# Half of chunk 1's h by seven half-size products, with weight sums moved to GpSimd

## The chip, the cores and the metric

The kernel runs on one core of one Trainium2 chip. The metric is the device time of that core in microseconds; the kernel before takes 255.4 us, the median of 3 runs that lie between 255.4 and 255.65. A profile is one further execution, recorded by the hardware.

Engine names in the profile: PE is TensorE (PEld its weight loads), DVE is VectorE, ACT is ScalarE, POOL is GpSimd, SP is SyncE, which issues most transfers.

## The reference

Linear attention for 8 batches of 8 heads, 576 rows and 64 columns, and a two-layer network on its result:

```
q_s = softmax(q, axis=-1);  k_s = softmax(k, axis=2)        # q, k, v: (8, 8, 576, 64)
kv  = einsum('bhsd,bhse->bhde', k_s, v)
x   = einsum('bhsd,bhde->bhse', q_s, kv) -> (4608, 512)
h   = x @ w_in                                              # w_in: (512, 2048)
g   = 0.5 * h * (1 + erf(h / sqrt(2)))
out = g @ w_out                                             # w_out: (2048, 512)
```

## The kernel before, in words

**Chunks.** The 576 rows of each batch are cut into 512 and 64. Chunk c (0 to 7) is the 512 rows of batch c; chunk 8 is the 64 rest rows of all batches. A chunk passes through: exponentials of q and k on ScalarE (`exp_q`, `exp_k`), casts of v to bf16 (`cast_v`), 72 small products for kv (`kv_mm`), the scaling of q by its sums (`norm_q`, or `q_sums` and `q_scale` apart), a transposition of q (from batch 2 on by a transposing DMA, `xbar_step`), the product x (`x_mm`, evacuated to `xT`), then h (L393 or L513), gelu, and y (L799).

**h.** xT has 512 contraction rows (4 blocks of 128) and 512 tokens; h has 16 tiles of 128 features, in the program's order t. In a *plain* tile (`h_mm`, `h_gelu`) four products of 512 columns go to one PSUM bank, and one ScalarE gelu moves it to `g`. Tiles t and t + 8 make a pair. Chunks 0 and 1 are all plain. From chunk 2 on, `h_waves` makes h in four groups (q = 0 to 3) of two pairs each by Strassen's scheme in Winograd's form: seven products of half the rows and half the tokens instead of eight. A product is four instructions of 256 columns. It needs sums of blocks of xT (`x_sums`, t1 to t4, on VectorE), sums of blocks of w_in made once (`quad_weights`, s1 to s4 for each half of the groups), and sums of the products:

- mm(1) into bank A, copied on as C (`seed`); mm(5) into bank B, copied to SBUF as r (`p5_copy`)
- mm(6) added to A; `e_sum`: B = A + r on VectorE; mm(2) added to C, whose gelu follows
- mm(7) added to A, after `e_sum` has read A; `r_sum`: r = A + r on VectorE, whose gelu follows
- mm(3) added to B, mm(4) to A after `r_sum` has read A; gelus of A and B

**y.** It uses the same scheme on g and w_out. Sums of blocks of g (`s_parts` and `s_ops`, VectorE) are made as pairs become ready; the mixed blocks of w_out (`mix_wo`, blocks 1, 3, 4, 6 and 7, each in two halves) once. `y_phase` runs seven products of 16 instructions in the order 4, 5, 1, 2, 3, 6, 7 (from chunk 2 on 3 follows 4; from chunk 3 to 7 product 3 is again split, class `Two`, whose weights are made by `weights(0)` and `weights(1)` on GpSimd). Between its products stand the steps of later batches, given as lists by place.

**Order.** Each engine runs its instructions in the order in which the program records them; the order is written out by hand. Semaphores make an instruction wait for what it reads or overwrites, and what is behind it on its engine waits too.

**Around the change.** In chunk 1 (L1150 to L1200) four plain tiles (8, 0, 9, 1) are made by hand, beside chunk 0's last evacuations and x. VectorE then mixes four half blocks of w_out (L1168 to L1171). `h_pairs` makes the other six pairs plain, with `s_ops` for every two pairs, and between them the w_in sums of the second half of the groups (`sums[0]` to `sums[2]`) on VectorE and the casts of batch 2's v on ScalarE. Then follow `exp_q(2)` and `exp_k(2)`, and `y_phase(1)`, in which batch 2's q is scaled and transposed, its kv made, batch 3's exponentials taken, and chunk 2's x made. Chunk 2's `h_waves` has `q_late` in its middle, which scales batch 3's q on GpSimd, issues its transposition and makes `weights(1)`.

Of the kernel before, what the change touches and what calls it, by code (L numbers as in the profile page):

```python
# [16 lines left out]
def kernel(  # L17
# [20 lines left out]
    J = 4  # L38
# [119 lines left out]
                in_=q[b, :, M:S, :].rearrange("h p d -> p h d"),  # L158
            )

    def exp_q(b, parts=1):

        e = attn_sb.tile([128, J, H, D], BF16, tag="eq")
        st[b]["eq"] = e
        dst = e.rearrange("p j h d -> p h j d")
        src = st[b]["qf"]
        if b == B:
            src = src.rearrange("p j h d -> p h j d")
        else:
            src = src.rearrange("p h (j d) -> p h j d", j=J)  # L170
        if parts == 1:
            sets = [(slice(i, None, 4), slice(u, None, 4)) for i, u in ((0, 0), (1, 1), (2, 3), (3, 2))]
        else:
            sets = []
            for h in (0, 4):
                sets += [(slice(h + i, h + i + n), slice(h + u, h + u + n))
                         for i, u, n in ((0, 0, 2), (2, 3, 1), (3, 2, 1))]
        for i, u in sets:
            nc.scalar.activation(out=dst[:, i], in_=src[:, u], func=AF.Exp)  # L179
# [221 lines left out]
    def s_parts(c, p0, n, which):  # L401


        g = st[c]["g"]
        a, b = slice(p0, p0 + n), slice(p0 + HK, p0 + HK + n)
        lo, hi = slice(0, HT), slice(HT, M)
        tt = nc.vector.tensor_tensor
        if 0 in which:
            tt(out=s5[:, a], in0=g[:, a, lo], in1=g[:, b, lo], op=ALU.add)
        if 1 in which:  # L410
            tt(
                out=s12[:, a].rearrange("p k (u m) -> p k u m", u=2),
                in0=g[:, a].rearrange("p k (u m) -> p k u m", u=2),
                in1=g[:, b, hi].unsqueeze(2).to_broadcast([128, n, 2, HT]), op=ALU.add,
            )
# [3 lines left out]
        if 2 in which:  # L419
            tt(out=g[:, a, hi], in0=g[:, a, hi], in1=g[:, a, lo], op=ALU.subtract)  # L420
            tt(out=g[:, b, lo], in0=g[:, b, lo], in1=g[:, b, hi], op=ALU.subtract)  # L421

    def s_ops(c, p0, n):
# [19 lines left out]
    def tt(out, in0, in1, op=ALU.add, eng=nc.vector):  # L443
        eng.tensor_tensor(out=out, in0=in0, in1=in1, op=op)  # L444

    quad = {"s": {}}

    def quad_weights(w):

        q = quad["s"][w] = wst.tile([128, 4, 2, 512], BF16, tag=("w4", "w1")[w], name="quad_s")  # L450
        up, dn = slice(w * 512, w * 512 + 512), slice((w + 2) * 512, (w + 3) * 512)
        a11, a12 = wi_bf[:, 0:2, up], wi_bf[:, 2:4, up]
        a21, a22 = wi_bf[:, 0:2, dn], wi_bf[:, 2:4, dn]
        s1, s2, s3, s4 = (q[:, i] for i in range(4))
        return [
            lambda: tt(s1, a21, a22), lambda: tt(s2, s1, a11, ALU.subtract),
            lambda: tt(s3, a11, a21, ALU.subtract), lambda: tt(s4, a12, s2, ALU.subtract),
        ]
# [19 lines left out]
    def h_waves(c, mid, sums=None):  # L478

        h_begin(c)
# [9 lines left out]
        if mid:  # L492
            bank_of.update(B=("kv0", "kv1") * 2, C=("x1", "x2") * 2)
        held = {}

        def take(kind, q):
            held[kind, q] = bank(roles[bank_of[kind][q]], "q" + kind.lower(), (128, 2, HT))

        def mm(m, *qs):
            for q in qs:  # L500
# [29 lines left out]
        def r_sum(q):  # L530
            tt(held["r", q], held["A", q], held["r", q])
# [5 lines left out]
                nc.scalar.activation(out=g[:, t:t + 2, half], in_=held[kind, q], func=AF.Gelu)  # L537

        vcopy, scopy = nc.vector.tensor_copy, nc.scalar.copy
        mm(1, 0, 1)  # L540
        seed(0)
        if mid:
# [10 lines left out]
            mm(6, 0, 1)  # L553
            e_sum(0)
            e_sum(1)
            mid()
            mm(2, 2, 3)
            gelu("C", 2, 3)
            mm(7, 0, 1)
            r_sum(0)  # L560
            r_sum(1)
            mm(3, 0, 1)
            gelu("B", 0, 1)
            mm(6, 2)
# [129 lines left out]
    class Two:  # L694
# [11 lines left out]
        def weights(self, part):  # L706

            W = wo_bf[:, UP, HN:DM].rearrange("p (a h b) n -> p h a b n", h=2, b=2)
            b11, b12, b21, b22 = (W[:, i, :, :, j:j + 128] for i in range(2) for j in (0, 128))
            o = [self.w[:, i].rearrange("p (a b) n -> p a b n", b=2) for i in range(5)]  # L710
            eng = nc.gpsimd
            if part == 0:
                tt(o[0], b11, b22, eng=eng)
                tt(o[1], b12, b22, ALU.subtract, eng=eng)
                return
            tt(o[2], b21, b11, ALU.subtract, eng=eng)
            tt(o[3], b11, b12, eng=eng)
            tt(o[4], b21, b22, eng=eng)
            w = self.w[:, 4]
            eng.tensor_scalar(out=w, in0=w, scalar1=-1.0, scalar2=None, op0=ALU.mult)  # L720

# [56 lines left out]
    def y_phase(c, ins, p3=None):  # L778
# [30 lines left out]
        if p3:  # L809
            p3.mm(c, bx, (4, 5, 1), True)  # L810
            p3.snap(bx)
        mm(4, bd, True)
        if c > 1:
            nc.scalar.copy(out=f, in_=bd)
            after(8)
            if p3:
                p3.mm(c, bx, (2, 3, 6, 7), False)
            else:
                mm(3, bx, True)
            nc.scalar.copy(out=c12, in_=two(bx))  # L820
            after(9)
        else:
            nc.vector.tensor_copy(out=f, in_=bd)
        after(0)
        if p3:
            p3.corner2(c12)
# [165 lines left out]

    w16 = None

    def mix_wo(m, a):


        lo, hi = slice(0, HN), slice(HN, DM)
# [10 lines left out]
        nc.vector.tensor_tensor(out=o, in0=i0, in1=i1, op=op)  # L1009

    def warm(n, z):
        ps = psum_y.tile([128, DM], FP32, tag="y")
# [269 lines left out]
```

## Time and profile before

| | |
|---|---|
| median of 3 runs | 255.4 us |
| the profiled execution, its time | 255.87 us |
| its span, first to last instruction | 253.9 us |
| TensorE busy | 247.9 us, 98% |
| VectorE busy | 219.1 us, 86% |
| ScalarE busy | 190.4 us, 75% |
| GpSimd busy | 102.8 us, 40% |
| chunk 1's h, by the chain | 44.1 to 58.5 us |
| y of chunk 1, with batch 2's kv | 58.5 to 71.6 us |
| chunk 2's h | about 72.9 to 85.3 us |

How to read it: the busy share of TensorE counts matmuls whose ends are modelled, so the chain of waits, followed back from the last instruction, says better what holds the end. A line of it has the start, the length, the engine, what was written, the line of the kernel, and how many instructions were merged. In the timeline a line has the start, the time from the first start to the last end, the engine, line, operation, what was written from what, sizes and count; in brackets the idle time before it and what ended it. A line of stretches has, for each engine, busy time and count, then the granted TensorE clock, the share of the DMA engines and GB/s.

### The profile page before, as it was taken

How to read it: one execution, taken by the hardware profiler on the slowest of the kernel's cores; microseconds unless marked ns; L12 is line 12 of the kernel's file. 1: busy time of each engine (PE TensorE's matmuls, PEld its weight loads, DVE VectorE, ACT ScalarE, POOL GpSimd, SP SyncE). 2: the span in 40 equal slices, each digit the busy share in tenths (PEclk: the TensorE clock that was granted, in tenths of full speed). 3: DMA queues.
4: the chain of work that ended last, by engine and by line, in shares of the span. 5: the costliest groups of instructions: out<-in, count | busy, mean ns of one | idle time of the engine just before them, and what ended most of it. 6: DMA issues, size and time to landing. Idle time of an engine off the chain costs nothing.

```text
span 253.9 us, 6825 instructions
## 1 busy us (share of the span) xinstructions
PE 247.9 (98%) x2738; PEld 196.1 (77%) x2738; DVE 219.1 (86%) x395; ACT 190.4 (75%) x326; POOL 102.8 (40%) x177
## 2 busy tenths in 40 slices
PE   7999999999999999999999999999999999999994
PEld 3444444448888888898889988998889889988883
DVE  1878898788987997998999899989999999868972
ACT  4785978699977996889688968896887788248711
POOL 1530023000978459106950596059603960560000
PEclk9999999999999999999999999999999999999998
DMA  7999999995329999890569255810520061004033
GB/s 239 397 367 420 405 406 400 401 407 206 61 64 288 375 265 377 246 340 5 188 196 310 98 188 177 204 36 3 165 87 3 1 193 57 3 4 165 0 84 84
DMA packets 43168, 50.24 MB, mean 198 GB/s; under 512 B 20225, under 2 KB 30465, under 8 KB 42881
## 3 DMA queue, kind: packets, MB, share of 16 engines
q1 hardware_dynamic: 42416, 49.13, 57.8%
q10 hardware_dynamic: 720, 0.69, 1.0%
q8 instruction: 21, 0.34, 0.6%
q14 instruction: 11, 0.08, 0.1%
HBM read 36.70 MB, written 9.44 MB: 182 GB/s over the span
## 4 chain that ended last, share of the span: by engine, by line
PE 81%; DMA 16%; DVE 1%; SPq 0%; issue 0%
PE qa L513 19%; PE ya L799 10%; PE qb L513 10%; PE yd L799 10%; DMA f<-in_q_dram 7%; PE ye L799 6%; PE ps L393 6%; PE yb L799 5%; PE qc L513 5%; DMA w<-in_moe_w_out_dram 3%; DMA w<-in_moe_w_in_dram 3%; PE yx L753 3%; DMA f<-in_v_dram 2%; PE kv L231 2%; PE ps L359 1%; PE ya L882 1%
## 5 line engine op out<-in xcount | busy, mean ns | idle before, releaser
L513 PEld LDWEIGHTS <-quad_s 128*128 128x128 bf16 x448 | 43.8, 98 | 5.1
L799 PEld LDWEIGHTS <-g 128*128 128x128 bf16 x368 | 35.2, 98 | 4.8 <-issue 0.4
L513 PEld LDWEIGHTS <-wi_bf 128*128 128x128 bf16 x336 | 32.8, 98 | 3.9
L799 PEld LDWEIGHTS <-s 128*128 128x128 bf16 x336 | 32.7, 98 | 3.7
L513 PE MATMUL qa<-quad_t,quad_s 128*128 128x256 bf16 x224 | 29.2, 273 | 0.0
L275 POOL TENSOR_TENSOR e<-e,recq 128x1024 bf16<-128x1024 bf16 (+1 forms) x4 | 9.3, 2330 | 47.8 <-DVE recq L270 41.0
L393 PE MATMUL ps<-xT,wi_bf 128*128 128x512 bf16 x128 | 28.1, 379 | 0.2 <-DVE kvc L244 0.2
L444 POOL TENSOR_TENSOR y_sb<-y_sb 128x128 f32<-128x128 f32 x56 | 26.0, 498 | 2.8 <-issue 2.8
L269 DVE TENSOR_REDUCE qsum<-e 128x16 f32<-128x1024 bf16 (+1 forms) x12 | 20.9, 1746 | 6.8 <-ACT e L179 6.5
L284 POOL TENSOR_TENSOR e<-e,recq 128x256 bf16<-128x256 bf16 x40 | 24.7, 653 | 1.8 <-DVE recq L270 1.2
L393 PEld LDWEIGHTS <-wi_bf 128*128 128x128 bf16 x128 | 12.4, 98 | 15.3 <-issue 0.7
L521 ACT COPY qc<-qa 128x512 f32<-128x512 f32 x26 | 13.9, 577 | 11.4 <-PE qa L513 5.3
L399 ACT ACTIVATE g<-ps 128x512 bf16<-128x512 f32 x32 | 17.6, 602 | 6.1 <-PE ps L393 5.8
L179 ACT ACTIVATE e<-f 128x512 bf16<-128x512 f32 (+1 forms) x42 | 20.5, 556 | 2.1 <-DMA f<-in_q_dram 1.9
L537 ACT ACTIVATE g<-r 128x512 bf16<-128x512 f32 x28 | 17.3, 631 | 6.3 <-DVE r L444 6.3
L444 DVE TENSOR_TENSOR qb<-qa,r 128x512 f32<-128x512 f32 x28 | 18.1, 691 | 4.1 <-PE qa L513 1.6
L537 ACT ACTIVATE g<-qc 128x512 bf16<-128x512 f32 x28 | 15.2, 594 | 7.4 <-PE qc L513 7.4
L418 DVE TENSOR_TENSOR s<-g 128x1024 bf16<-128x1024 bf16 x28 | 19.8, 726 | 0.0
L196 POOL CAST v_aug<-f 128x576 bf16<-128x576 f32 x25 | 17.0, 711 | 4.4 <-DMA f<-in_v_dram 4.3
L444 DVE TENSOR_TENSOR r<-qa,r 128x512 f32<-128x512 f32 x28 | 17.9, 680 | 0.7 <-PE qa L513 0.7
L184 ACT ACTIVATE ek<-f 128x2304 bf16<-128x2304 f32 (+1 forms) x10 | 17.2, 1734 | 1.2 <-DMA f<-in_k_dram 1.2
L1213 POOL CAST scr<-g 128x1 f32<-128x1 bf16 x4 | 0.7, 187 | 42.3 <-DVE g L421 42.3
(117 smaller groups left out, 550.2 us busy)
## 6 DMA issues: line engine op xcount, KB each, us to landing
out_dram<-y_sb SPq DMA_DIRECT2D x16, 512.0 KB, 3.9
f<-in_k_dram SPq DMA_DIRECT2D x6, 1152.0 KB, 9.5
f<-in_v_dram SPq DMA_DIRECT2D x6, 1152.0 KB, 10.5
f<-in_q_dram SPq DMA_DIRECT2D x6, 1024.0 KB, 7.6
w<-in_moe_w_in_dram SPq DMA_DIRECT2D x6, 512.0 KB, 8.9
f<-in_v_dram SPq DMA_DIRECT2D x8, 288.0 KB, 6.5
f<-in_q_dram SPq DMA_DIRECT2D x4, 512.0 KB, 9.0
w<-in_moe_w_out_dram SPq DMA_DIRECT2D x2, 1024.0 KB, 11.4
```

What stands on the lines that cost most here:

```text
L179: nc.scalar.activation(out=dst[:, i], in_=src[:, u], func=AF.Exp)
L184: nc.scalar.activation(out=ek[b % 2][:, i:i + n], in_=st[b]["kf"][:, i:i + n].rearrange("p x (n d) -> p x n d", n=NS), func=AF.Exp,)
L196: eng.tensor_copy(out=o, in_=i)
L269: nc.vector.reduce_sum(out=qsum, in_=st[b]["eq"][:, :, i * w:(i + 1) * w, :], axis=AX.X)
L284: nc.gpsimd.tensor_tensor(out=e, in0=e, op=ALU.mult, in1=st[b]["recq"][:, j, i:i + 4].unsqueeze(2).to_broadcast([128, 4, D]),)
L393: nc.tensor.matmul(ps, wi_bf[:, dm, t * 128:(t + 1) * 128], st[c]["xT"][:, dm, :], start=(dm == 0), stop=(dm == NDM - 1),)
L399: nc.scalar.activation(out=st[c]["g"][:, t, :], in_=ps, func=AF.Gelu)
L418: tt(out=s12[:, a, half], in0=g[:, a, half], in1=g[:, b, hi], op=ALU.add)
L444: eng.tensor_tensor(out=out, in0=in0, in1=in1, op=op)
L513: nc.tensor.matmul(held[kind, q][:, u], w, mov[m][:, k], start=(m in (1, 5) and u == 0 and k == 0), stop=(k == 1), skip_group_check=True,)
L537: nc.scalar.activation(out=g[:, t:t + 2, half], in_=held[kind, q], func=AF.Gelu)
L799: nc.tensor.matmul(ps[:, j * HN:(j + 1) * HN], act[m][:, k, j * 128:(j + 1) * 128], wgt[m][:, k, :], start=(first and k == 0 and j == 0), ...
```

## The change

- Chunk 1's tiles 2, 3, 10 and 11 (pairs 2 and 3) stay plain, now inside `h_waves`. Pairs 4 to 7 become groups 2 and 3 of `h_waves`, with the products in the order 5, 1, (plain pair 3), 6, 2, 7, 3, 4.
- All four block sums of w_in for these groups go to GpSimd, each in four pieces of 128x256: sums 0 and 2 ahead of the scaling of batch 1's q, sums 1 and 3 after the last plain tiles made by hand. So do the mixed half blocks 7, 4, 1 and 3 of w_out, in four pieces each, and after them the casts of batch 2's v.
- `x_sums(1)` is made on VectorE. `s_ops` of pairs 2 and 3 stands after plain pair 3, ahead of `e_sum`. The sums of pairs 4 to 7 are made together after the last gelus, one of them (part 6) later in `y_phase(1)`.
- `exp_q(2)` is cut in two halves around the copy of the first y product, which goes from VectorE to ScalarE; `exp_k(2)` follows. In the program they stand inside `y_phase(1)`.
- Batch 3's q is summed and scaled in two halves, the second in chunk 2's `h_waves` after `r_sum(1)`, and then transposed. `weights(1)` goes from `q_late` to the beginning of chunk 3, in pieces of half the size.

```diff
@@ quad_weights(w, parts=None)
+        if parts:
+            def tt(out, in0, in1, op=ALU.add):
+                for k in range(2):
+                    for n in (slice(0, 256), slice(256, 512)):
+                        nc.gpsimd.tensor_tensor(out=out[:, k, n], in0=in0[:, k, n], in1=in1[:, k, n], op=op)
+        else:
+            tt = two_block_sum
@@ h_waves
+        first_banks = {"A": (5, 6), "B": (1, 7), "C": (3, 4)}
+
+        def plain(p):
+            for i, t in ((2, p + HK), (0, p)):
+                ps = bank(i)
+                h_mm(c, ps, t, range(NDM))
+                h_gelu(c, ps, t)
...
+        if c == 1:
+            plain(2)
+            for q in (2, 3):
+                mm(5, q)
+                mm(1, q)
+            seed(2)
+            seed(3)
+            p5_copy(2, vcopy)
+            p5_copy(3, vcopy)
+            plain(3)
+            s_ops(c, 2, 2)
+            mm(6, 2, 3)
+            e_sum(2)
+            e_sum(3)
+            mm(2, 2, 3)
+            gelu("C", 2, 3)
+            mm(7, 2, 3)
+            r_sum(2)
+            r_sum(3)
+            gelu("r", 2, 3)
+            mm(3, 2, 3)
+            mm(4, 2, 3)
+            gelu("A", 2, 3)
+            gelu("B", 2, 3)
+            s_parts(c, 4, 4, (0,))
+            s_parts(c, 4, 4, (3,))
+            s_parts(c, 4, 4, (4,))
+            s_parts(c, 4, 4, (5,))
+            return
...
-            mid()
+            mid[0]()
             mm(2, 2, 3)
             gelu("C", 2, 3)
             mm(7, 0, 1)
             r_sum(0)
             r_sum(1)
+            mid[1]()
@@ Two.weights
-            tt(o[2], b21, b11, ALU.subtract, eng=eng)
-            tt(o[3], b11, b12, eng=eng)
-            tt(o[4], b21, b22, eng=eng)
+            for a in range(2):
+                tt(o[2][:, a], b21[:, a], b11[:, a], ALU.subtract, eng=eng)
+                tt(o[3][:, a], b11[:, a], b12[:, a], eng=eng)
+                tt(o[4][:, a], b21[:, a], b22[:, a], eng=eng)
@@ y_phase
+        if c == 1:
+            exp_q(2, parts=2, part=0)
         mm(4, bd, True)
...
-            nc.vector.tensor_copy(out=f, in_=bd)
+            nc.scalar.copy(out=f, in_=bd)
+            exp_q(2, parts=2, part=1)
+            exp_k(2)
@@ mix_wo(m, a, parts=False)
+        if parts:
+            for i in range(4):
+                nc.gpsimd.tensor_tensor(out=o[:, i], in0=i0[:, i], in1=i1[:, i], op=op)
+        else:
+            nc.vector.tensor_tensor(out=o, in0=i0, in1=i1, op=op)
@@ chunk 1
-    sums = quad_weights(1)
+    sums = quad_weights(1, parts=True)
+    sums[0]()
+    sums[2]()
     mix_wo(6, 0)
...
-    mix_wo(7, 1)
-    mix_wo(4, 1)
-    mix_wo(1, 1)
-    mix_wo(3, 1)
+    sums[1]()
+    sums[3]()
+    for m in (7, 4, 1, 3):
+        mix_wo(m, 1, parts=True)
+    cast_v_all(2)
...
-    h1 = {p + 3: [lambda p=p: cast_v(2, p, nc.scalar)] for p in range(HP)}
-    h1[1] = [sums[0]]
-    h1[3] += sums[1:3]
-    h_pairs(1, h1, done=t1s, turn=Banks(2, 0, 5, 6))
-
-
-    exp_q(2, parts=2)
-    exp_k(2)
+    x_sums(1, (1, 2, 3, 4))
+    s_ops(1, 0, 2)
+    h_waves(1, None)
...
     y_phase(1, {
-        0: [sums[3]],
         7: [lambda: norm_q(2, 0, 2)],
-        1: [lambda: norm_q(2, 1, 2, nc.vector)],
+        1: [lambda: norm_q(2, 1, 2, nc.vector), lambda: s_parts(1, 4, 4, (6,))],
         2: [lambda: cast_v_all(3), first_weights, lambda: xbar_step(2), lambda: exp_q(3)],
-        3: [lambda: kv_step(2), lambda: exp_k(3), lambda: q_sums(3)],
+        3: [lambda: kv_step(2), lambda: exp_k(3), lambda: q_sums(3, 0, 2)],
...
-        q_scale(3, nc.gpsimd)
+        q_scale(3, nc.gpsimd, 0, 2)
+
+    def q_later():
+        norm_q(3, 1, 2)
         xbar_step(3)
-        y3.weights(1)
...
-        h_waves(c, q_late if c == 2 else None, p3 and p3.sums)
+        if c == 3:
+            y3.weights(1)
+        h_waves(c, (q_late, q_later) if c == 2 else None, p3 and p3.sums)
```

More of the change, by code (lines that the diff above doesn't have):

```diff
@@ L159, in load_qrest, with exp_q @@
             )
-    def exp_q(b, parts=1):
-        e = attn_sb.tile([128, J, H, D], BF16, tag="eq")
-        st[b]["eq"] = e
+    def exp_q(b, parts=1, part=None):
+        if part != 1:
+            st[b]["eq"] = attn_sb.tile([128, J, H, D], BF16, tag="eq", name="e")
+        e = st[b]["eq"]
         dst = e.rearrange("p j h d -> p h j d")
@@ L174, in exp_q @@
             sets = []
-            for h in (0, 4):
+            for h in (0, 4) if part is None else (4 * part,):
                 sets += [(slice(h + i, h + i + n), slice(h + u, h + u + n))
@@ L418, in s_parts @@
                 tt(out=s12[:, a, half], in0=g[:, a, half], in1=g[:, b, hi], op=ALU.add)
-        if 2 in which:
+        if 2 in which or 5 in which:
             tt(out=g[:, a, hi], in0=g[:, a, hi], in1=g[:, a, lo], op=ALU.subtract)
+        if 2 in which or 6 in which:
             tt(out=g[:, b, lo], in0=g[:, b, lo], in1=g[:, b, hi], op=ALU.subtract)
@@ L444, in tt, with quad_weights @@
         eng.tensor_tensor(out=out, in0=in0, in1=in1, op=op)
+    two_block_sum = tt
     quad = {"s": {}}
-    def quad_weights(w):
+    def quad_weights(w, parts=None):
         q = quad["s"][w] = wst.tile([128, 4, 2, 512], BF16, tag=("w4", "w1")[w], name="quad_s")
@@ L478, in h_waves @@
     def h_waves(c, mid, sums=None):
-        h_begin(c)
+        if c > 1:
+            h_begin(c)
         g, xT = st[c]["g"], st[c]["xT"]
@@ L494, in h_waves @@
         held = {}
+        first_banks = {"A": (5, 6), "B": (1, 7), "C": (3, 4)}
[4 more added lines that the diff above has]
+                h_gelu(c, ps, t)
         def take(kind, q):
-            held[kind, q] = bank(roles[bank_of[kind][q]], "q" + kind.lower(), (128, 2, HT))
+            i = first_banks[kind][q - 2] if c == 1 else roles[bank_of[kind][q]]
+            held[kind, q] = bank(i, "q" + kind.lower(), (128, 2, HT))
         def mm(m, *qs):
@@ L993, with mix_wo @@
     w16 = None
-    def mix_wo(m, a):
+    def mix_wo(m, a, parts=False):
         lo, hi = slice(0, HN), slice(HN, DM)
@@ L1008, in mix_wo @@
         }[m]
-        nc.vector.tensor_tensor(out=o, in0=i0, in1=i1, op=op)
+        if parts:
[3 more added lines that the diff above has]
+            nc.vector.tensor_tensor(out=o, in0=i0, in1=i1, op=op)
     def warm(n, z):
```

## The prediction

> **What bounds the kernel now.** I read the page first, then the chain of waits in order of time, then the timeline of the stage that changes.
>
> ```profile
> PE 247.9 (98%) x2738; PEld 196.1 (77%) x2738; DVE 219.1 (86%) x395; ACT 190.4 (75%) x326; POOL 102.8 (40%) x177
> PE 81%; DMA 16%; DVE 1%; SPq 0%; issue 0%
> ```
>
> The chain that ends last is 81% TensorE. In order of time it leaves DMA and VectorE at 44.12 us and then holds TensorE alone to 250.34:
>
> ```profile
> 45.48 13.06 PE ps L393 x60
> 58.54 1.75 PE yd L799 x16
> ...
> 63.78 1.75 PE yd L799 x16
> 65.52 0.76 PE kv L231 x72
> ...
> 75.67 0.87 PE qb L513 x8
> 76.55 0.87 PE qa L513 x8
> ```
>
> So behind 44 us a product saved is time saved, and every gap that opens on TensorE is time lost: nothing hides it. Eight products of 256 columns take 0.87 us (0.109 each); the 60 of 512 columns are 0.216 apart by their starts.
>
> The stage in question on the other engines (start, duration, then the work):
>
> ```profile
> 51.67 0.60 ACT L399 ACTIVATE g<-ps 128x512 bf16<-128x512 f32 x1 [0.27 <-PE ps L393]
> 52.30 0.43 DVE L409 TENSOR_TENSOR s<-g 128x512 bf16<-128x512 bf16 x1 [0.48 <-ACT g L399]
> 52.64 0.68 DVE L411 TENSOR_TENSOR s<-g 128x1024 bf16<-128x1024 bf16 x1
> 53.36 0.42 DVE L420 TENSOR_TENSOR g<-g 128x512 bf16<-128x512 bf16 x1
> 53.70 0.42 DVE L421 TENSOR_TENSOR g<-g 128x512 bf16<-128x512 bf16 x1
> 54.03 0.68 DVE L444 TENSOR_TENSOR quad_s<-quad_s,wi_bf 128x1024 bf16<-128x1024 bf16 x1
> ```
> ```profile
> 59.19 1.28 ACT L179 ACT_TABLE_LOAD   x1
> 60.48 2.38 ACT L179 ACTIVATE e<-f 128x512 bf16<-128x512 f32 x6
> 62.76 2.11 ACT L184 ACTIVATE ek<-f 128x2304 bf16<-128x2304 f32 x1
> 65.45 0.83 PE L231 MATMUL kv<-v_aug,ek 64*64 64x65 bf16 x72
> 77.17 1.29 DVE L444 TENSOR_TENSOR qb<-qa,r 128x512 f32<-128x512 f32 x2
> ```
>
> To see: the four VectorE sums of one pair of plain tiles start 0.03 us after the tile's gelu and hold VectorE for 1.73 us (52.30 to 54.03); exp_k(2) ends at 64.87, only 0.58 us ahead of the kv products that read it.
>
> **The change part by part.** Terms are in us against the profiled execution (span 253.9, time 255.87, so 1.97 lie around the span); its time is 0.47 over the median 255.4, and I put the sum on the median.
>
> *1. Products.* Tiles of pairs 4 to 7 were 8 x 4 products of 512 columns, 32 x 0.216 = 6.91. They become two groups of seven products in four pieces, 56 x 0.109 = 6.12. **-0.8**.
>
> *2. mm(7) waits for e_sum behind s_ops.* The new VectorE order is s_ops(1,2,2), then e_sum(2), e_sum(3). mm(7) adds into the bank that e_sum reads, so it waits. TensorE before: the first product of the last 60 starts at 45.41. After: 20 products of 512 to 49.74, four groups of four halves (4 x 0.437) to 51.49, plain(3) (8 x 0.216) to 53.21, mm(6) and mm(2) (2 x 0.874) to 54.96, where mm(7) would start. VectorE: plain(3)'s last product starts at 53.00 and runs 0.38, its gelu follows 0.04 later (both as the tile ahead of the gelu at 50.80 shows), 53.41 to 54.01; the four sums run 54.05 to 55.78 (1.73 as above), e_sum(2) 0.69 to 56.47, TensorE 0.07 behind it: 56.54. Lost 1.58, and 0.16 more, as e_sum(3) ends 0.60 later and half of mm(7) takes 0.44. **+1.74**. Queued behind mm(7) on TensorE is everything that follows.
>
> *3. GpSimd beside those sums.* GpSimd gets 8 + 16 more pieces of 128x256 from 42.4 on (its last cast of v_aug now ends at 42.38). The nearest rows are its e pieces of the same shape, 8 in 4.80, 0.6 each, so it works till 56 at least, over both s_ops. What such pieces do to a VectorE sum with both inputs in SBUF:
>
> ```profile
> 94.28 4.80 POOL L284 TENSOR_TENSOR e<-e,recq 128x256 bf16<-128x256 bf16 x8 [0.57 <-ACT ek L184]
> 97.62 0.42 DVE L444 TENSOR_TENSOR quad_t<-xT 128x512 bf16<-128x512 bf16 x1
> 98.77 0.60 DVE L444 TENSOR_TENSOR quad_t<-xT,quad_t 128x512 bf16<-128x512 bf16 x1
> ```
>
> 0.00 and 0.18 over the 0.42 that it takes alone; in later chunks the same sums beside the same pieces take 0.60 to 0.89, +0.47 at most. Four sums stand ahead of e_sum: 0 to 1.9; I take 0.28 each, the middle of what is seen, **+1.1**. The Trainium skill (SBUF — State Buffer, "Who interferes with whom") goes further: a VectorE instruction with two SBUF inputs and a GpSimd one that reads SBUF exclude each other for whole instructions. By that each sum could wait for a whole piece, 4 x 0.6 = 2.4, and the total would be 260.3; the 0.42 row agrees less than the 0.89 ones. x_sums(1) meets the pieces too, but has 47.6 against 49.7 to spare. GpSimd's own results come in time: mixed block 4 ends near 54 (used from 57), block 3 near 59 (used at 67), cast_v(2) near 63 (used at 67).
>
> *4. exp_k(2) comes late.* ACT must first finish gelu A and B of groups 2 and 3, which need mm(4), the last product ahead of the y stage (start T). By the pitch of 0.55 for such gelus the last ends at T+1.9. Then the table (1.28), half of exp_q(2) (1.14), the copy of yd, now ACT's (0.47 until the next starts), the other half (1.14), exp_k (2.11): T+8.1. TensorE reaches kv at T + 64 x 0.109 = T+7.0 (before: 65.45 with T 58.4). **+1.15**, with 1.0 to 1.4 as ends. The copy of yd ends at T+4.9, just ahead of mm(2) at T+5.2, which writes that bank. Behind, ACT needs 6.56 from exp_k's end to the end of the next gelu table (64.87 to 71.43), TensorE 6.1 from kv to the x products and 0.5 to their end: no second gap. norm_q(2) ends near T+9.5 and its transposing DMA (2.27 at 66.64) at T+12, for x products at T+14. Where this stall goes, nothing else is late by these rows.
>
> *5. Sums 0 and 2 of w_in on GpSimd at 30.4 to 36.* GpSimd idled 19.96 there. Beside it VectorE has three sums and a cast, then a q scaling that must wait for GpSimd's own (it took 1.72 beside one, 1.23 alone): about +1.4 at 38.1. VectorE idled 1.04 and 0.19 for DMA at 40.36 and 40.98, and its work from there is on the chain until 44.08. Ends 0 and 0.6; **+0.25**.
>
> *6. VectorE and ACT freed.* Four mixes (0.69 each), four w_in sums, and four v casts on ACT (0.66) go. None was on the chain: nothing, since TensorE covers it.
>
> *7. Batch 3's q.* q_sums(3) in halves: the second (1.22 + 0.25) falls in chunk 2 where VectorE idled 1.46 ahead of e_sum: 0 to 0.1, nothing taken. The scaling on GpSimd (3.62) becomes 2 x 1.90, the second from 81.6, so the transposing DMA is issued about 3 us later than at 80.75; it took 9.24 beside 3 loads, and x needs it 95.7. The loads behind it on SP (90.03) are for the next batch's exp, 20 us later. Nothing; without that cover at most 3.
>
> *8. y3's weights(1) in chunk 3.* Six pieces and 1.49 from 102.8 to about 109, used at 111.1. They lie beside five VectorE sums ahead of e_sum, up to 0.3 each, against slack of 0.36 idle and 0.30 to mm(7): 0 to 0.7, **+0.15**.
>
> Sum: -0.8 + 1.74 + 1.1 + 1.15 + 0.25 + 0.15 = +3.6; 255.4 + 3.6 = **259.0**.
>
> **The rivals.**
>
> *Faster.* If mm(7) found its e_sum done at 54.96 and kv its exp_k at T+7, only term 1 is left: 254.6. That needs e_sum 1.6 us earlier than VectorE's order allows, or ACT 1.1 us shorter. For it: VectorE and ACT lose work in this stage, and both waits are worked out, not seen. Against it: VectorE is in order, and the gelu it waits for is itself behind TensorE, so a late or early stage moves both ends together. 0.05; a mix that ends within 0.5 us of before, 0.03.
>
> *One wait alone.* Terms 2 and 3 without 4 and the small ones: 255.4 - 0.8 + 2.8 = 257.4; bare term 2 alone: 256.3; term 4 alone, 255.8, which is no change. For it: terms 3, 5 and 8 rest on contention that some rows do not show. 0.12.
>
> *Whole pieces.* Each of the four sums waits for one whole GpSimd piece of 0.6: 259.0 - 1.1 + 2.4 = 260.3. For it the rows of 0.89, against it the row of 0.42 beside a piece. 0.12. (It is what the Trainium skill's rule in term 3 gives.)
>
> *The clock.* A gap of 2.8 us on TensorE has no example between 44 and 250 us, but the end has one:
>
> ```profile
> 250.30:252.00 1.70, 0.02 (x1) 0.00 (x0) 0.29 (x1) 0.00 (x0) 0.00 (x0) 1.00 0.66 162
> 252.00:253.90 1.90, 0.00 (x0) 0.00 (x0) 0.00 (x0) 0.00 (x0) 0.00 (x0) 0.63 0.21 50
> ```
>
> The granted clock (third figure from the end) averages 0.63 in the last stretch, so it fell to half some 2.1 us after the last product. If it falls in the gap, and stays for as long as it was low at the start at most (products from 1.44; 5 us), half of that is lost: 259.0 + 2.6 = 261.6. The Trainium skill (TensorE: Matmul & The Clock Gate, Part 1) asks for an idle window of about 3.4 us first, which speaks against it here; the 2.1 us speak for it. 0.10.
>
> **How the numbers follow.** Forecast 0.58; whole pieces 0.12; the clock 0.10; one wait alone 0.12; within 0.2% 0.03; faster 0.05. 0.2% is 0.5 us, about what a measurement of this kernel can tell from no change. Faster 0.05, same 0.03, slower 0.92. The forecast's own ends: low 255.4 - 0.8 + 1.74 + 0 + 1.0 = 257.3, high with 1.9, 1.4, 0.6 and 0.7 260.9. The range reaches to the middle of one wait alone below, 256.9, and to 261.2 above.
>
> **What would show it.** In the changed profile's chain: products of chunk 1 end 0.8 earlier by their sum; TensorE idle of 1.7 to 3.6 ahead of the second qa of groups 2 and 3, released by VectorE qb; idle of about 1.15 ahead of the kv products, released by ACT ek; s_ops rows over 0.42 and 0.68 beside GpSimd; granted clock at 1.00 there. The prediction is wrong if e_sum runs ahead of s_ops(1,2,2), if mm(7) starts within 0.5 us of mm(2)'s end, or if ek ends before TensorE has reached kv.

## The result, and the profile after

The changed kernel takes 263.5 us (median of 4 runs, 261.9 to 263.9) against 255.4 (4 runs, 255.38 to 255.65): a ratio of 1.030, 95% interval 1.026 to 1.035. So it is slower, by 8.1 us where 3.6 were forecast. The profiled execution took 263.85 us, with a span of 262.0. Now and then an execution takes about twice as long, whatever the kernel (519.6 us was seen); such executions are in none of the times here.

The page of the changed kernel, busy times, the granted clock in 40 slices, and the chain by engine:

```profile
PE 249.0 (95%) x2757; PEld 198.7 (76%) x2762; DVE 228.6 (87%) x391; ACT 190.2 (73%) x325; POOL 134.2 (51%) x217
PEclk9999997999999999999999999999999999999999
PE 82%; POOL 5%; ACT 5%; DMA 4%; DVE 2%; issue 1%; SPq 0%; POOLq 0%; ACTq 0%
```

GpSimd and ScalarE were not on the chain before; now they hold 5% each. DMA's 16% on the old chain is 4%: the work ahead of 44 us ends last on another engine. The clock dips in the seventh slice, at 39 to 46 us.

The chain of waits of the changed kernel, in order of time, at the places where it is not TensorE:

```profile
30.56 5.82 POOL quad_s L463 x6
36.66 1.29 POOL quad_s L463 x2
37.95 2.84 POOL e L276
40.79 2.15 POOL v_aug L197 x2
...
61.14 0.62 DVE qb L446
61.81 0.61 PE qa L533 x4
...
70.58 2.02 ACT ek L185
72.64 0.83 PE kv L232 x71
```

Three places: GpSimd's new sums of w_in ahead of chunk 1, e_sum ahead of mm(7), exp_k(2) ahead of kv. A table of TensorE's landmarks, by the starts of its instructions, shows what each is worth:

| us | before | after | lost there |
|---|---|---|---|
| first of the long run of 512-column products in chunk 1's h | 45.41 | 49.01 | 3.60 |
| first product of y | 58.37 | 64.58 | 2.61 |
| batch 2's kv | 65.45 | 72.64 | 0.98 |
| chunk 2's h | 72.81 | 80.00 | 0.00 |
| chunk 3's h | 98.72 | 105.94 | 0.03 |
| x products of chunk 4 | 121.36 | 129.38 | 0.80 |
| span | 253.9 | 262.0 | 0.08 |

The first row is the surprise. The changed kernel's timeline of that stage (start, duration, then the work), VectorE and then GpSimd:

```profile
31.07 1.69 DVE L1044 CAST wo_bf<-w 128x2048 bf16<-128x2048 f32 x1
32.80 2.11 DVE L1068 TENSOR_TENSOR w<-wo_bf 128x1024 bf16<-128x1024 bf16 x2
38.95 3.45 DVE L1068 TENSOR_TENSOR wo_bf<-wo_bf 128x1024 bf16<-128x1024 bf16 x2
42.33 1.69 DVE L1044 CAST wo_bf<-w 128x512 bf16<-128x512 f32 x2
...
30.56 7.39 POOL L463 TENSOR_TENSOR quad_s<-wi_bf 128x256 bf16<-128x256 bf16 x8 [15.31 <-ACT wo_bf L1046]
37.91 2.88 POOL L276 TENSOR_TENSOR e<-e,recq 128x1024 bf16<-128x1024 bf16 x1
40.74 3.00 POOL L197 CAST v_aug<-f 128x576 bf16<-128x576 f32 x3
```

The same instructions in the kernel before:

```profile
30.99 1.22 DVE L989 CAST wo_bf<-w 128x2048 bf16<-128x2048 f32 x1
32.25 1.29 DVE L1009 TENSOR_TENSOR w<-wo_bf 128x1024 bf16<-128x1024 bf16 x2
38.04 1.28 DVE L1009 TENSOR_TENSOR wo_bf<-wo_bf 128x1024 bf16<-128x1024 bf16 x2
35.14 1.90 POOL L275 TENSOR_TENSOR e<-e,recq 128x1024 bf16<-128x1024 bf16 x1 [19.96 <-DVE recq L270]
```

Each is longer beside the other engine, and each makes the next overlap that was not there: the eight pieces take 7.39 us, so GpSimd's scaling of q starts 2.77 us later and takes 2.88 for 1.90; it holds VectorE's mixes (3.45 for 1.28); then the casts of v lie beside the casts of w_out. TensorE, which has only short work here (transpositions, 64-wide kv products), waits three times for GpSimd, 2.0 us in all; its timeline in the changed kernel:

```profile
40.84 0.71 PE L324 MATMUL tp<-identity,e 64*64 64x64 bf16 x64 [0.82 <-POOL e L276]
41.91 0.22 PE L232 MATMUL kv<-v_aug,ek 64*64 64x65 bf16 x2 [0.36 <-POOL v_aug L197]
42.98 0.61 PE L232 MATMUL kv<-v_aug,ek 64*64 64x65 bf16 x34 [0.86 <-POOL v_aug L197]
```

Then its clock falls to half, for 3.4 us. Stretches of the changed kernel (the third figure from the end is the granted clock):

```profile
43.10:44.80 1.70, 1.48 (x37) 0.81 (x34) 1.70 (x6) 0.13 (x1) 1.70 (x3) 0.51 1.05 411
44.80:46.50 1.70, 1.70 (x5) 0.44 (x3) 0.89 (x3) 0.19 (x1) 1.70 (x4) 0.50 1.04 411
```

Three of the kernels below have the same work and much the same waits here, and in their profiles the clock does not fall. One of them, with exp_k(2) moved:

```profile
41.80:43.90 2.10, 0.89 (x58) 0.63 (x46) 2.10 (x3) 1.58 (x2) 2.10 (x3) 1.00 1.09 398
43.90:46.50 2.60, 2.60 (x48) 1.35 (x48) 2.60 (x8) 1.10 (x3) 2.60 (x5) 1.00 1.04 411
```

In these three the long run starts 6.66 us after the first transposition, in the changed kernel 8.17, in the kernel before 5.46. So the fall of the clock is 1.5 of the 3.60 us, and the waits are the other 2.1.

The stage that the prediction was about, again from the timeline of the changed kernel: plain(3)'s gelu, the four sums, e_sum, the pieces on GpSimd beside them, and the product that waits; then exp_k(2) and kv.

```profile
57.01 0.60 ACT L400 ACTIVATE g<-ps 128x512 bf16<-128x512 f32 x1 [0.27 <-PE ps L394]
57.64 0.81 DVE L410 TENSOR_TENSOR s<-g 128x512 bf16<-128x512 bf16 x1
58.38 1.15 DVE L412 TENSOR_TENSOR s<-g 128x1024 bf16<-128x1024 bf16 x1
59.56 0.77 DVE L421 TENSOR_TENSOR g<-g 128x512 bf16<-128x512 bf16 x1
60.26 0.88 DVE L423 TENSOR_TENSOR g<-g 128x512 bf16<-128x512 bf16 x1
58.13 3.54 POOL L1066 TENSOR_TENSOR wo_bf<-wo_bf 128x256 bf16<-128x256 bf16 x4
61.81 1.20 PE L533 MATMUL qa<-quad_t,quad_s 128*128 128x256 bf16 x8 [3.08 <-DVE qb L446]
...
70.48 2.11 ACT L185 ACTIVATE ek<-f 128x2304 bf16<-128x2304 f32 x1
72.64 0.83 PE L232 MATMUL kv<-v_aug,ek 64*64 64x65 bf16 x72 [0.91 <-ACT ek L185]
```

The sums are the forecast ones in the forecast place: 3.43 us from the first to e_sum's start, against 1.73 alone. Each takes 0.35 to 0.47 us more than its 0.42 or 0.68. e_sum, which reads one of its inputs from PSUM, takes its usual 0.69 beside a piece.

### The profile page after: what moved, and what is told of

Same layout as the page of the kernel before. It is cut to its first block, busy times and chain, and to the rows that moved or that the text cites. A ratio compares the mean times of both kernels' runs of the same rounds, so it can differ in the third digit from the quotient of the medians.

```text
span 262.0 us, 6914 instructions
## 1 busy us (share of the span) xinstructions
PE 249.0 (95%) x2757; PEld 198.7 (76%) x2762; DVE 228.6 (87%) x391; ACT 190.2 (73%) x325; POOL 134.2 (51%) x217
## 4 chain that ended last, share of the span: by engine, by line
PE 82%; POOL 5%; ACT 5%; DMA 4%; DVE 2%; issue 1%; SPq 0%; POOLq 0%; ACTq 0%
PE qa L533 19%; PE qb L533 10%; PE ya L850 9%; PE yd L850 8%; PE ps L394 8%; PE ye L850 5%; PE yb L850 5%; PE qc L533 5%; PE yx L804 3%; POOL quad_s L463 3%; PE kv L232 2%; DMA f<-in_v_dram 2%; PE ps L360 2%; DMA f<-in_q_dram 2%; PE ya L937 1%; POOL v_aug L197 1%
## 5 line engine op out<-in xcount | busy, mean ns | idle before, releaser
L533 PEld LDWEIGHTS <-quad_s 128*128 128x128 bf16 x480 | 46.9, 98 | 10.0 <-issue 4.1
L533 PE MATMUL qa<-quad_t,quad_s 128*128 128x256 bf16 x240 | 31.6, 272 | 3.4 <-DVE qb L446 3.4
L557 ACT ACTIVATE g<-r 128x512 bf16<-128x512 f32 x30 | 18.5, 631 | 10.8 <-DVE r L446 10.8
L557 ACT ACTIVATE g<-qc 128x512 bf16<-128x512 f32 x30 | 16.3, 594 | 8.2 <-PE qc L533 8.2
L197 POOL CAST v_aug<-f 128x576 bf16<-128x576 f32 x29 | 21.0, 758 | 1.1 <-DMA f<-in_v_dram 1.1
L446 DVE TENSOR_TENSOR qb<-qa,r 128x512 f32<-128x512 f32 x30 | 19.4, 690 | 2.1 <-PE qa L533 1.4
L394 PE MATMUL ps<-xT,wi_bf 128*128 128x512 bf16 x93 | 21.1, 379 | 0.1
L446 DVE TENSOR_TENSOR r<-qa,r 128x512 f32<-128x512 f32 x30 | 19.2, 681 | 0.8 <-PE qa L533 0.6
L276 POOL TENSOR_TENSOR e<-e,recq 128x1024 bf16<-128x1024 bf16 x5 | 10.5, 2098 | 15.9 <-DVE recq L271 9.4
L400 ACT ACTIVATE g<-ps 128x512 bf16<-128x512 f32 x24 | 12.8, 603 | 5.8 <-PE ps L394 5.8
```

Of the source, the lines that this page charges most:

```text
L197: eng.tensor_copy(out=o, in_=i)
L394: nc.tensor.matmul(ps, wi_bf[:, dm, t * 128:(t + 1) * 128], st[c]["xT"][:, dm, :], start=(dm == 0), stop=(dm == NDM - 1),)
L533: nc.tensor.matmul(held[kind, q][:, u], w, mov[m][:, k], start=(m in (1, 5) and u == 0 and k == 0), stop=(k == 1), skip_group_check=True,)
```

## The experiments

Every edit is against the changed kernel unless the text says otherwise. A gap is the time between the starts of two neighbouring products across a wait; 0.11 or 0.20 is what stands there with no wait. A median mixes executions with and without the fall of the clock at 43 us, which is worth 1.5 us, so two profiles are compared from the start of the long run to the end as well: 213.0 us in the changed kernel.

### e_sum ahead of the sums

```diff
             plain(3)
-            s_ops(c, 2, 2)
             mm(6, 2, 3)
...
             r_sum(3)
+            s_ops(c, 2, 2)
```

> s_ops(1,2,2) is moved from ahead of e_sum to behind r_sum. Theory (mm(7) waits 3.25 us for e_sum, which is queued behind four sums that a gelu and GpSimd's pieces delay): the gap ahead of mm(7) is under 0.2, the time falls by 3.0 to 3.4, to about 260.3; up to 1 of it can come back ahead of product 5 of y, whose sums are now later. Rival (e_sum itself is late, through its other inputs or GpSimd): a gap of over 1 stays ahead of mm(7).

Measured: 260.9 us, ratio 1.021 (1.019 to 1.022). The gap ahead of mm(7) fell from 3.36 to 0.11, and kv's from 1.18 to 0.20. TensorE's timeline shows what came in their place:

```profile
62.14 0.60 PE L850 MATMUL ye<-wo_bf,s 128*128 128x256 bf16 x4
64.14 1.48 PE L850 MATMUL ye<-wo_bf,s 128*128 128x256 bf16 x12 [1.40 <-DVE s L410]
```

Product 5 of y reads the sums that now end later. So the wait for e_sum is what the prediction says it is, and taking it away hands 1.57 us of it to the next reader of VectorE's work, with 0.44 more ahead of chunk 2's x and 0.7 by the start of chunk 3's h. In this profile the clock stayed at 1.00 and the long run of products began at 48.12: 0.9 earlier than with the clock's dip. From there to the end it is 1.9 us shorter than the changed kernel; that much is the edit's, and the rest of the 2.6 is not.

### The w_in sums back on VectorE

```diff
+        v = two_block_sum
-            lambda: tt(s1, a21, a22), lambda: tt(s2, s1, a11, ALU.subtract),
-            lambda: tt(s3, a11, a21, ALU.subtract), lambda: tt(s4, a12, s2, ALU.subtract),
+            lambda: v(s1, a21, a22), lambda: tt(s2, s1, a11, ALU.subtract),
+            lambda: v(s3, a11, a21, ALU.subtract), lambda: tt(s4, a12, s2, ALU.subtract),
...
-    sums[0]()
-    sums[2]()
```

Sums 0 and 2 are made in chunk 1's h instead.

> Sums 0 and 2 of w_in leave GpSimd's stretch at 30 us; VectorE makes them in chunk 1's h. Theory (these eight pieces hold the engines' shared access to SBUF, so that batch 1's q, the w_out casts and all behind them come late, TensorE idles and its clock falls to half at 43.1): the 512-column products after the x step start at 45.4 to 45.7 instead of 49.0, the clock stays at 1.00, and the time falls by 3.3 to 3.6, to about 260.0. Rival (the clock falls by itself, in any gap of this stretch, and contention costs little): the clock still falls and the time stays above 261.5. Rival (the stretch is late because of something else in the change): start stays near 49.0, time 263.5.

263.7 us (262.65 to 263.94). A second set of runs has the profile:

> The same edit as in the run that gave no gain (sums 0 and 2 of w_in by VectorE in chunk 1's h), for a profile at the full clock. First theory (contention at 30 us delays all): the products after the x step start at 45.4 to 45.7. If they do and the time still is near 263.7, the 3.6 are lost again inside chunk 1's h or y, because GpSimd's sums 1 and 3 now wait for sum 0 and its mixed blocks end some 5 later: a gap ahead of y's products 4 or 1, or of kv, of 3 in all. Rival (the lateness has nothing to do with these sums): start near 48 to 49.

262.5 us, ratio 1.027 (1.025 to 1.030). The long run of products starts at 45.25 us, 45.41 in the kernel before: so the two GpSimd sums are the whole of the 3.60 us, and both expectations have the start right and the time wrong. For y starts at 64.51, where it started at 64.58. The two sums now stand in VectorE's queue at 46.0 and 49.4 us (0.68, and 1.15 beside GpSimd), ahead of both s_ops; e_sum comes at 58.7, the gap ahead of mm(7) is 4.76 us, and there the clock falls. TensorE's timeline of this kernel:

```profile
59.44 1.87 PE L534 MATMUL qa<-quad_t,quad_s 128*128 128x256 bf16 x8 [4.48 <-DVE qb L446]
```

The same kernel's stretches around it, with the granted clock third from the end:

```profile
57.20:59.00 1.80, 0.00 (x0) 0.00 (x0) 1.80 (x3) 0.00 (x0) 1.80 (x3) 0.77 1.02 414
59.00:64.90 5.90, 5.46 (x26) 3.90 (x26) 2.36 (x4) 2.00 (x4) 5.90 (x11) 0.50 0.15 58
65.10:67.00 1.90, 1.90 (x20) 1.71 (x18) 1.62 (x2) 1.88 (x4) 1.90 (x3) 1.00 0.00 0
```

At half the clock the eight products take 1.87 us for 1.04. Up to y the longer gap costs 1.4 us and the half clock 2.3, which is the gain again. It is one execution, and the slowest of its four: its mean clock is 0.987, and the other three, with 0.992 or 0.993, took 262.3 to 262.5.

### The mixed blocks: on VectorE, and on GpSimd whole

```diff
     for m in (7, 4, 1, 3):
-        mix_wo(m, 1, parts=True)
+        mix_wo(m, 1)
```

> The four mixed half blocks of w_out go back to VectorE, all else as in the change. Theory (beside GpSimd's pieces each VectorE sum with two inputs in SBUF waits for one piece, 0.47 each): GpSimd is done with its sums at 48.9, the four sums of s_ops(1,2,2) take 1.73 instead of 3.43, the gap ahead of mm(7) is 1.6 instead of 3.25, and the time falls by 1.5 to 1.7, to about 262.0. Rival (the long gap is VectorE's own order alone): VectorE has 2.4 more to do ahead, the gap stays at 3.2 or grows.

```diff
-            for i in range(4):
-                nc.gpsimd.tensor_tensor(out=o[:, i], in0=i0[:, i], in1=i1[:, i], op=op)
+            nc.gpsimd.tensor_tensor(out=o, in0=i0, in1=i1, op=op)
```

> The same four mixed half blocks stay on GpSimd, each as one instruction of 128x1024 instead of four of 128x256. Theory (the engines exclude each other for whole instructions): VectorE's x_sums and s_ops each wait for a whole block of about 2.5, so that e_sum comes 3 to 4 later than in the change: the gap ahead of mm(7) is 6 to 7 and the time about 267. Rival (they share the access in proportion): the gap stays near 3.2, the time near 263.5.

On VectorE: 262.1 us, 1.025 (1.023 to 1.027). With GpSimd away from the four sums they take what they took before, and the gap ahead of mm(7) is 1.68. VectorE and TensorE in its timeline:

```profile
58.45 0.42 DVE L410 TENSOR_TENSOR s<-g 128x512 bf16<-128x512 bf16 x1
58.80 0.69 DVE L412 TENSOR_TENSOR s<-g 128x1024 bf16<-128x1024 bf16 x1
59.52 0.42 DVE L421 TENSOR_TENSOR g<-g 128x512 bf16<-128x512 bf16 x1
59.86 0.42 DVE L423 TENSOR_TENSOR g<-g 128x512 bf16<-128x512 bf16 x1
60.94 1.19 PE L533 MATMUL qa<-quad_t,quad_s 128*128 128x256 bf16 x8 [1.41 <-DVE qb L446]
```

This cuts the wait in two: 1.68 - 0.11 = 1.57 is the order (term 2 had 1.58), and 3.36 - 1.68 = 1.68 is GpSimd (term 3 had 1.1). The mixes are not free on VectorE either: x_sums(1) come behind them, and the gap ahead of mm(5) is 1.04 instead of 0.22. From the start of the long run on, this kernel is 0.9 us shorter than the changed one, not the 1.5 to 1.7 expected. That its median lies at the expected 262.0 is luck: three of its four runs had a mean clock of 1.000, of the changed kernel's only one.

Whole instructions on GpSimd: 268.5 us, 1.050 (1.047 to 1.053), and 7.56 ahead of mm(7), both more than expected. In that gap the clock falls, and stays low from 62.18 to 69.00 us, which costs 2.1 us up to y. The same work in four instructions instead of sixteen, GpSimd and VectorE in its timeline:

```profile
55.59 2.30 POOL L1065 TENSOR_TENSOR wo_bf<-wo_bf 128x1024 bf16<-128x1024 bf16 x1
55.84 2.34 DVE L410 TENSOR_TENSOR s<-g 128x512 bf16<-128x512 bf16 x1
```

A sum of 0.42 us takes 2.34: it ends 0.29 us after GpSimd's instruction does (57.89). In the changed kernel the sums of 128x512 beside the short pieces likewise end 0.28 us after a piece does. So these two kinds of instruction take turns, whole instruction by whole instruction; what the short pieces buy is a shorter turn.

### exp_k(2) ahead of the second half of exp_q(2)

```diff
-            nc.scalar.copy(out=f, in_=bd)
-            exp_q(2, parts=2, part=1)
+            nc.vector.tensor_copy(out=f, in_=bd)
             exp_k(2)
+            exp_q(2, parts=2, part=1)
```

(with the copy of yd back on VectorE)

> exp_k(2) goes ahead of the second half of exp_q(2), and the copy of yd back to VectorE. Theory (kv waits 1.0 us for exp_k, the last of a row of ScalarE work): that gap goes, but the row is as long as before up to the gelu table, so 0.3 to 0.5 comes back ahead of chunk 2's first products, which wait for ScalarE's xT: net 0.5 to 0.7 less, about 262.9. Rival (kv waits for GpSimd's v casts or for something else): the gap of 1.0 stays.

263.2 us, 1.030 (1.027 to 1.034): no gain (213.0 us from the start of the long run to the end, as in the changed kernel), though kv's gap is 0.20. VectorE's sums and scaling of the later half of q are late instead, and what stands behind them; TensorE's timeline of this kernel:

```profile
75.27 1.91 PE L850 MATMUL ya<-w,g 128*128 128x256 bf16 x16 [0.54 <-DVE y_sb L446]
77.61 0.63 PE L360 MATMUL ps<-qT,kvc 64*64 64x512 bf16 x8 [0.44 <-DVE recq L271]
```

### weights(1) back in chunk 2

```diff
+        y3.weights(1)
...
-        if c == 3:
-            y3.weights(1)
```

(in `q_late`'s second part, behind the transposition)

> weights(1) goes back from the beginning of chunk 3 to chunk 2's middle, behind the transposition. Theory (beside it VectorE's sums ahead of e_sum in chunk 3 take longer, and mm(7) of groups 2 and 3 waits 0.5 there, and 0.1 in y): these gaps go, 0.6 less, about 262.9. Rival (it is q's later scaling that delays chunk 3): the gap of 0.5 stays.

264.5 us, 1.036 (1.032 to 1.041). Chunk 3's gap of 0.61 falls to 0.11, so these pieces are its cause. In chunk 2 they meet VectorE's sums of g (1.04 to 1.15 instead of 0.68 from 92.0 to 97.4), and product 5 of y stands 1.41 us for the last of them. From chunk 2's h to the end the profile is 0.7 us longer; the median is 1.0 longer, with one run in which the clock fell further (mean 0.981, 266.75 us).

### All places given another order

Undoing one part at a time moved the loss; so the next kernel keeps the half-size products and gives each place another order at once: the w_in sums on VectorE; on GpSimd only mixes 7 and 4 ahead of the sums, mixes 3 and 1 and the casts of v each behind a one-element copy that holds them until a VectorE step is done; all s_ops of chunk 1 behind r_sum; the copy of yd back on VectorE and kv later; the second half of batch 2's q scaled by GpSimd; weights(1) in two parts, both in chunk 2. The text that follows says two things that the edit does not do: exp_k(2) stays behind exp_q(2), and starts earlier only because the copy has left ScalarE; and mixes 3 and 1 wait for a copy of r, only the casts for g.

```diff
+            mid()
+            plain(2, 0)
             mm(6, 2, 3)
...
+            plain(3 + HK, 2)
             gelu("B", 2, 3)
+            plain(3, 0)
+            s_ops(c, 0, 3)
...
+    def late_mixes():
+        nc.gpsimd.tensor_copy(out=scr[:, 2:3], in_=quad["r"][:, 2, 0, 0:1])
+        for m in (3, 1):
+            mix_wo(m, 1, parts=True)
+        sums[3]()
...
-        3: [lambda: kv_step(2), lambda: exp_k(3), lambda: q_sums(3, 0, 2)],
-        10: [lambda: table(AF.Gelu)],
+        3: [lambda: exp_k(3)],
+        10: [lambda: kv_step(2), lambda: q_sums(3, 0, 2), lambda: table(AF.Gelu)],
```

> The half-size products are kept, and each of the places where the changed kernel loses time is given another order at once: w_in's block sums on VectorE; on GpSimd only mixes 7 and 4 ahead of the sums of chunk 1, and mixes 3 and 1 behind g's copy; s_ops(1,2,2) behind the sums of r; exp_k(2) ahead of the rest of exp_q(2), with kv_step(2) three products later; weights(1) of chunk 3 in pieces, with its negation late. Theory (the added time is the sum of four waits, each with its own cause, and nothing else): none of the four gaps is left, the products of 512 columns start at 44.5 to 45.5 us, the granted clock is 1.0, and the time is before's less the 0.8 us of products, give or take 0.5 for what the moved work delays: 254.1 to 255.6. Rival (VectorE, at 87% of the span, has no room for the added work in any order, so that a wait taken away in one place comes back in another, as in the runs that undid one part): new gaps of 0.5 to 1.5 us ahead of product 4, product 5 or kv, and 257 to 261.

257.4 us, 1.007 (1.006 to 1.008). The four gaps are gone and the clock is at 0.999: the long run starts at 45.34 and y at 57.55, 12.21 us later, where it was 12.96 in the kernel before: 0.75 of the products' 0.8. Then a new gap of 2.01 us stands ahead of chunk 2's x:

```profile
72.54 0.63 PE L360 MATMUL ps<-qT,kvc 64*64 64x512 bf16 x8 [1.74 <-DMA qT<-e]
```

The transposing DMA waits for the scaling of q that this kernel had put on GpSimd (to 68.66). Two more steps went after that, each an edit of the kernel of the step before.

```diff
-        1: [lambda: norm_q(2, 1, 2), lambda: s_parts(1, 4, 4, (6,))],
+        1: [lambda: norm_q(2, 1, 2, nc.vector), lambda: s_parts(1, 4, 4, (6,))],
```

> The rearranged kernel with one line changed: the second half of batch 2's q is scaled by VectorE (65.7 us), not by GpSimd (66.6 to 68.7 us). Theory (the 2.01 us ahead of the x products of chunk 2 are the transposition by DMA, which starts only when GpSimd has scaled that half, and GpSimd's additions to y, pushed into the sums of chunk 2's x, double those sums): the gap falls to 0.2, the two small gaps of 0.17 and 0.27 in chunk 2's h go, and the time is 257.4 - 1.8 - 0.4 = 255.2 (254.8 to 255.8), not slower than before. Rival (VectorE is full there, and 1.3 us more on it delays s_parts 6 and the evacuation ahead of product 7): the gap moves to product 7 of y with 0.5 to 1.3 us, and 256.2 to 257.2.

256.7 us, 1.0045 (1.003 to 1.006): the transposition was issued at 67.8 instead of 68.7 and 1.23 us of the gap were left, with 0.26 new ahead of product 7: between the two expectations.

```diff
+            cast_v(2, 0, nc.scalar)
...
+            cast_v(2, 1, nc.scalar)
...
-            nc.vector.tensor_copy(out=f, in_=bd)
+            nc.scalar.copy(out=f, in_=bd)
             exp_q(2, parts=2, part=1)
```

(two of batch 2's casts go behind chunk 1's `plain(2, 0)` and `gelu("C", 2, 3)`; the others stay on GpSimd)

> The rearranged kernel with q's second half on VectorE, and three pieces of work given to ScalarE in chunk 1: two of the four casts of batch 2's v (in its idle time at 52 and 54 us) and the copy of yd (between the halves of exp_q(2)). Theory (the 1.23 us ahead of chunk 2's x are VectorE's lateness: 0.7 us of copy and 0.47 of taking turns with GpSimd in the scaling of q): the transposition starts at 66.9 us and not at 67.8, the gap of 0.26 ahead of product 7 goes, and the time is 256.7 - 0.9 - 0.2 = 255.6 (255.1 to 256.0), level with the kernel before. Rival (ScalarE's chain is now the late one: exponentials of q and k, two copies and a table load up to 71.8 us): x's evacuation or the kv products wait for ScalarE instead, a new gap of 0.4 to 0.7 us, and 256.2 to 256.8.

256.0 us (255.3 to 256.6 in 12 runs), 1.0012 (1.0001 to 1.0023): level with the kernel before. VectorE was early, as meant: the transposition was issued at 66.38, before 66.64 in the kernel before. In the profiled execution it then took longer, SyncE's queue first and TensorE second:

```profile
66.38 3.84 SPq L340 DMA_TRANSPOSE qT<-e  x1
72.35 0.63 PE L360 MATMUL ps<-qT,kvc 64*64 64x512 bf16 x8 [1.69 <-DMA qT<-e]
```

It landed 5.8 us after its issue, 4.3 in the kernel of the step before. The trace shows where the time went: the transposition's packets began at 67.64, and none began from 68.25 to 69.58, while one packet of 16 KB of the queue that fetches instructions ran from 67.61 to 69.59. Stretches of the same kernel (the second figure from the end is the DMA engines' share):

```profile
68.25:69.58 1.33, 1.33 (x15) 1.20 (x13) 1.29 (x4) 1.33 (x2) 1.25 (x3) 1.00 0.10 0
69.58:71.80 2.22, 1.08 (x10) 0.72 (x8) 1.72 (x4) 1.94 (x3) 2.22 (x4) 1.00 0.81 178
```

In the step before, that packet was over at 69.50, beside the transposition's first ones (from 69.09), and there was no such pause. This is one execution of twelve, and no run tests the fetch; the 1.3 us between the fastest and the slowest run of this kernel are of the size of the pause, but that it is their cause is only argued. So the time came out at the upper end of what was expected, and in this profile without the shorter wait that was to bring it. No version here is faster than the kernel before.

## Why the prediction was wrong in size

Direction and chain were right: slower, by waits of TensorE for VectorE and ScalarE, with the two that it named in their places. The size was 8.1 us instead of 3.6, outside the range. By its own terms:

| term | forecast | measured | by what |
|---|---|---|---|
| 1 products | -0.8 | -0.8 | y start less the other losses; -0.75 bare in the rearranged kernel |
| 2 order of e_sum | +1.74 | +1.73 | gap 1.68 without GpSimd, less 0.11, and 0.16 for the second half |
| 3 GpSimd beside the sums | +1.1 | +1.68 | 3.36 less 1.68 |
| 4 exp_k(2) late | +1.15 | +0.98 | 1.18 less 0.20 |
| 5 w_in sums on GpSimd | +0.25 | +3.60 | long run 49.01 against 45.41; 45.25 with the sums taken away |
| 8 weights(1) | +0.15 | +0.80 | chunk 3: gap 0.61 instead of 0.11, 0.16 for the second half of mm(7), short waits in y |

They add to 7.99, and the spans differ by 8.1. Without the fall of the clock, in the run that took 261.9 us, the time still lies above the range.

**The step that failed is term 5.** It let the eight pieces run from 30.4 to 36 us in idle time of GpSimd, and gave VectorE 1.4 us of delay, most of it covered by VectorE's own idle time. Three things in it were wrong. First, it priced what GpSimd does to VectorE (there, in term 3) but not what VectorE does to GpSimd: the pieces took 7.39 us, to 37.95. Even an end at 36 would have lain in GpSimd's own scaling of q, which began at 35.14. Second, it let the delay end at the first step: in truth each late instruction came to lie beside another one of the other engine (q's scaling, the mixes, the casts), which was late again. Third, it looked for the delay on VectorE, with its 1.04 and 0.19 us of idle time, while the chain shows that TensorE waited for GpSimd's own scaling (to 40.79) and casts of v. That contention is 2.1 us of the 3.60, by the three profiles without a fall of the clock; the other 1.5 is the clock, which the term did not have at all.

**Term 3** was mis-sized within its ends: 0.35 to 0.47 for a sum, not 0.28. The row of 0.42 beside a piece, which held the estimate down, gave no bound, as that sum can have fallen between two pieces. The Trainium skill (SBUF — State Buffer, "Who interferes with whom") says that such instructions block each other for their whole length; the runs agree, with a sum of 0.42 us that took 2.34 beside a piece of 2.30. What the rule as I used it had too high was the price: a sum waited 0.35 to 0.47 for a piece of 0.67 (alone), so for what was left of the piece in progress, not all of it. The rival made from it, 260.3, lay nearer to the result than the forecast, but by a loss of 4.1 ahead of mm(7), where it was 3.4.

**Term 4** came out by its own row of ScalarE work: exp_k(2) ended 8.0 us after y's start, where it had 8.1. One reading in it was wrong without harm here: it counted batch 2's transposition as over 2.27 us after its issue, which is how long SyncE took to issue it; it landed 4.2 us after. In the changed kernel that left 0.7 us ahead of chunk 2's x (78.06 against 78.75), and in the rearranged kernels it is the wait that remains.

**The clock** was a rival with the wrong place and the wrong condition. In the gap of 3.36 us ahead of mm(7), for which it was priced, it did not fall. In every profile here it changes only a whole number of steps of 3.413 us after its first rise: in the changed kernel at 5.60, and 11 and 12 steps later at 43.14 and 46.56. The step from 39.73 to 43.14 held all three waits, 2.0 us of idle time. In the two other profiles where the clock fell at 43 us (mixes on VectorE, weights(1) back) the step had 2.0 and 1.7; in the three where it did not, the same waits lay across a step's end at 41.6 to 41.8, with at most 1.2 us on either side. The gap of 3.36 us was cut in the same way, at 60.21, into 1.5 and 1.6 us. The first rise comes at 5.0 to 7.7 us, and differs from execution to execution of the same work, so whether these waits cost 1.5 us more turns on where the steps lie. All six profiles agree with this; no run tests it by moving the waits. Of the changed kernel's own runs, the one whose mean clock was 1.000 took 261.9, the three at 0.993 263.2 to 263.9. Where the gap was 4.76 us, 3.2 of them filled most of a step, and the clock stayed at half for two steps, 6.8 us.

**Terms 6 and 7** held: nothing from freed engines, and nothing from batch 3's q (chunk 2's h to chunk 3's h: 0.03).

The other mistake is of kind, not size. The terms were added as if each were one place; the runs show that most of them are one thing. By the profiles, taking away a wait gave 1.9 us of 4.2 (e_sum, with kv's), 0.9 of 1.7 (mixes), nothing of 1.0 (exp_k), and 0.7 less than nothing (weights(1)); the w_in sums gave 3.8 ahead of chunk 1's long run, and lost as much behind it. VectorE is 87% busy, and GpSimd's sums take time from it wherever they overlap.

## What to carry to other kernels

Work moved to a second engine is not free because that engine is idle: if both read two inputs from SBUF, count each overlapping pair twice, once for either engine, and follow the delay to the next overlap until an idle stretch really ends it. Price a moved step in the stage where it lands as carefully as in the stage that the change is about. And where one engine near its limit feeds a chain at several places, judge a cure by the next reader of that engine's results: here 0.8 us of saved products could be had on TensorE, but the first step behind them gave it back.

## What the runs showed of the hardware

- A VectorE sum with two SBUF inputs and a GpSimd sum alternate by whole instructions: 128x512 sums took 0.77 to 0.88 us instead of 0.42 beside GpSimd pieces of 128x256 (0.67 alone), 128x1024 sums 1.15 instead of 0.68, and the pieces 0.84 to 1.12. A sum with one input in PSUM took 0.69 beside them, as without. VectorE's cast of 128x2048 from fp32 took 1.69 instead of 1.22.
- The granted clock changed in steps of 3.413 us from its first rise, at a moment that differs from execution to execution. It fell to half at the end of steps with 1.7 to 2.0 us of idle time beside mostly short products, and of steps with 3.2 and 3.4 us, and not behind 1.5 and 1.6 us on either side of a step's end. Idle time alone does not settle it: with weights(1) back, a step ahead of mm(7) had 1.75 us, beside full-width products, and the clock stayed. What share of work keeps it up is open. The Trainium skill (TensorE: Matmul & The Clock Gate, Part 1) describes a free-running window of 3.4 us, and a fall after at least one idle window. The steps agree with the window. The fall at 43.14 does not agree with an idle one, as that step held 64 transpositions and 21 kv products of 65 columns; here the measurement decides.
- In one profile a transposition by DMA stood still for 1.3 us while the DMA engines fetched 16 KB of instructions.
